# Sliding-window attention with sinks ahead of four dense stages: two 128-column score blocks merged into one of 132

## The chip, the cores and the metric

The kernel runs on one core of one Trainium2 chip. The metric is the device time of one execution in microseconds (us); a smaller one is better. The engines of a core are named as in the profile: PE (TensorE, matrix products, with PEld for its weight loads), DVE (VectorE), ACT (ScalarE), POOL (GpSimd) and SP, which issues most DMAs. Each engine works through its own list of instructions in order.

## The reference

Two batches of 8 heads, 768 positions, 64 values per head. A query attends to the first 4 keys (the sinks) and to the 128 last keys up to its own; the numbers 4 and 128 come as inputs. Then four dense products follow, 512 wide outside and 1024 and 2048 wide inside.

```python
scores = scale * np.matmul(q, k.transpose(0, 1, 3, 2))
keep = is_sink | in_window
scores = np.where(keep, scores, -1000000000.0)
a = np.exp(scores - np.max(scores, axis=-1, keepdims=True))
a = a / (np.sum(a, axis=-1, keepdims=True) + 1e-09)
x = np.matmul(a, v)
h = (x @ w1) * (x @ w2) @ w3 @ w_out
g = softplus(h @ w_in)
out = g @ w_out2
```

## The kernel before

**Stages.** The attention comes first and leaves x for 1536 tokens. Then stage 1 (x times w1 and w2), stage 2 (w3 times w_out), stage 3 and stage 4 (the softplus layer) follow. In these, each fp32 number is split into two parts and each product is three matmuls (lines 153 to 155), which fill PE with matmuls of 512 columns. The weights come as 64-bit words and are decoded on ACT and DVE (lines 179 to 211); the first unit of w1 and w2 is decoded within the attention.

**Attention.** Heads go in pairs, 8 pairs in all, and each head has 6 tiles of 128 queries. For tile i the keys that can count are the 128 of the preceding block, the 4 sinks and the 128 of the tile's own block: 260 columns (`EW`), of which tile 0 uses the last 128. Per pair and tile `score` makes two matmuls, one for each head, into two PSUM tiles. Then per head and tile: `mask` (line 370, DVE) adds the mask, takes the minimum and moves the result to SBUF in one instruction, with a second short one that reads the minimum; `exp` (line 377, ACT) with the row sum; and, once all 6 tiles of a head are there, `total` and `inverse` (lines 383 and 387, DVE), `divide` (line 391, POOL), `turn` (line 403, PE: 11 transposes of 128x128 per head in 3 groups), `turned` (lines 413 and 415: the copy from PSUM, on DVE for g = 2 and, in even heads, g = 1, on ACT for the others), and `pv` (line 438, PE: 7 products per head in two PSUM banks, some of 256 columns and some of 128). The sinks of tiles 2 to 5 go a way of their own: `sink_copy` (POOL, lines 421, 422, 138), `sink_turn`, `sink_turned`, `sink_pv` (lines 447, 450, 457). `x_hi` and `x_lo` (lines 472 and 138) split the result.

**Order.** All these steps are given to a small planner (`Plan`), which writes one fixed order per engine before the program runs. It takes for each step the duration in ns in its `add`, latencies between engines, and a rank: the step's number plus 45 times its value in `PUT_OFF`. At each point it picks the step with the smallest start time plus 0.9 times its rank. So a large positive value sends a step behind others that could start some hundreds of ns later, and a negative one pulls it forward. A step that issues two instructions on DVE costs the planner the sum of the two that it is told. `score` of a tile waits for the masks of the tile before last (4 PSUM tiles), and the step kinds D (decode), vsh and vsl (sink values) and flag are fitted in between.

Of the kernel before, what the change touches and what calls it, by code (L numbers as in the profile page):

```python
# [9 lines left out]
F32 = mybir.dt.float32  # L10
FR = mybir.dt.float32r
# [9 lines left out]
P = 128  # L21
# [6 lines left out]
NSINK = 4  # L28
# [18 lines left out]
PUT_OFF = dict(  # L47
    vsh=1, vs=-20, vsl=-2, nw=-0.5, heat=3, D=16.4, flag=-1,
    S=-1.33, E=(0.31, 1.32), M=(0, -0.01), N=(0.61, 0.14), RC=(0.1, -0.58), C=(0.29, 0.2), T=(0.26, 0.18), P=(0.7, -1.01), K=(0.01, -0.3), PV=0.27, KT=-0.08, KC=-1.39, KV=0.51, XH=0.11, XL=-0.55,
)  # L50

PVS = ([(0, 0, 2), (1, 0, 2), (2, 0, 2), (3, 0, 1)], [(3, 1, 2), (4, 0, 2), (5, 0, 1)])

# [72 lines left out]
class Net:  # L126
# [116 lines left out]
    def mask_steps(self, pool):  # L243
# [4 lines left out]
        col = pool.tile([P, P], I32, name="col")  # L248
        inw, cur, snk, prev, k0, k1, self.m_0 = (
            pool.tile([P, P], F32, name=x) for x in ("inw", "cur", "snk", "prev", "k0", "k1", "m_0")  # L250
        )
        m_1, m_mid = self.m_1, self.m_mid = [pool.tile([P, EW], F32, name=x) for x in ("m_1", "m_mid")]

# [3 lines left out]
        def start():  # L257
            nc.gpsimd.iota(rel, pattern=[[-1, P]], base=0, channel_multiplier=1)
            nc.gpsimd.iota(col, pattern=[[1, P]], base=0, channel_multiplier=0)
            nc.gpsimd.memset(m_1[:, P:KB], -MASKED)  # L260

        return [
# [14 lines left out]
            ("m_0", "DVE", 135, lambda: bias(nc.vector, self.m_0, k0), ("km0",)),  # L277
            ("m_p", "Pool", 268, lambda: bias(nc.gpsimd, m_mid[:, 0:P], prev), ("prev",)),
            ("m_s", "Pool", 164, lambda: bias(nc.gpsimd, m_mid[:, P:KB], snk[:, 0:NSINK]), ("snk",)),
            ("m_c", "ACT", 160, lambda: nc.scalar.copy(m_mid[:, KB:EW], m_1[:, KB:EW]), ("m_1c",)),  # L280
        ]
# [31 lines left out]

    def sink_hi(self, pairs, j):
        if len(self.vshi) == j:
            self.vshi.append(self.ring.tile([P, B * NPAIR, P], FR, tag="u", name=f"vshi{j}", bufs=5))
        self.hi_pool(self.vshi[j][:, pairs], self.vsraw[j][:, pairs])
# [12 lines left out]
    def attention(self, pool, psum):  # L330
# [3 lines left out]

        bufs = dict(qk=3, v=3, e=4, st=4, pt=4)
        shape = dict(qk=[P, S + QT * KB], v=[P, QT, P], e=[P, QT, EW], st=[P, 3, QT], pt=[P, 2 * QT - 1, P])
        users = {}

        def buf(tag, h):

            if (tag, h) not in held:
                held[tag, h] = pool.tile(shape[tag], F32, tag=tag, name=f"{tag}{h}", bufs=bufs[tag])
            return held[tag, h]

# [10 lines left out]
        def tile_columns(i):  # L355
            return slice(KB, EW) if i == 0 else slice(0, EW)

        def score(pair, i):

            o, qk = tile_columns(i), buf("qk", pair)  # L360
# [28 lines left out]
        def divide(h, i):  # L389
            e = buf("e", h)[:, i, tile_columns(i)]  # L390
            nc.gpsimd.tensor_scalar(  # L391
                out=e, in0=e, scalar1=buf("st", h)[:, 2, i : i + 1], scalar2=1.0, op0=ALU.mult, op1=ALU.mult
            )

        def blocks(g):

            return [x for x in ((2 * g, 0), (2 * g, 1), (2 * g + 1, 0), (2 * g + 1, 1)) if x != (0, 0)]

        def turn(h, g):
            held["PT", h, g] = ps = psum.tile([P, 4, P], F32, tag="PT", name=f"ptp{h}_{g}", bufs=2)  # L400
            for j, (t, own) in enumerate(blocks(g)):
                c = slice(KB, EW) if own else slice(0, P)
                nc.tensor.transpose(ps[:, j, :], buf("e", h)[:, t, c], self.ident)

        def on_dve(h, g):

            return g == 2 or g == 1 and h % 2 == 0

        def turned(h, g):
            lo, n = max(4 * g - 1, 0), len(blocks(g))  # L410
            dst, src = buf("pt", h)[:, lo : lo + n, :], held.pop(("PT", h, g))[:, 0:n, :]
            if on_dve(h, g):
                nc.vector.tensor_copy(dst, src)
            else:
                nc.scalar.copy(dst, src)

        def sink_copy(h):
            sk = self.skb[(h // 2) % 2][0]
            src = buf("e", h)[:, 2:QT, P:KB]
# [12 lines left out]
        def pv(pair, bank):  # L432

            for n, (j, s0, s1) in enumerate(PVS[bank]):
                o = (j + s0) * P - bank * CH
                for par in range(2):
                    r = slice(par * D, par * D + D)
                    nc.tensor.matmul(
                        xt(pair, bank)[r, o : o + (s1 - s0) * P], buf("v", pair)[:, j, r],
                        buf("pt", 2 * pair + par)[:, 2 * j + s0 : 2 * j + s1, :],  # L440
                        start=n == 0, stop=False, skip_group_check=True,
                    )
# [64 lines left out]
        for pair in range(B * H // 2):  # L507
# [7 lines left out]
            for i in range(QT):  # L515
# [4 lines left out]
                add("S", "PE", 440 if i else 220, score, pair, i, after=need)  # L520
                m = [] if pair else [(x,) for x in (("m_0",), ("m_1p", "m_1c"), ("m_p", "m_s", "m_c"))[min(i, 2)]]
                for h in heads:
                    add("M", "DVE", 350 if i else 212, mask, h, i, after=[("S", pair, i), *free("e", h), *m])
                    add("E", "ACT", 496 if i else 385, exp, h, i, after=[("M", h, i)])
            users["qk", pair] = [("S", pair, i) for i in range(QT)]
            for h in heads:
                add("N", "DVE", 78, total, h, after=[("E", h, i) for i in range(QT)])
                add("RC", "DVE", 104, inverse, h, after=[("N", h)])
                for i in range(QT):
                    add("C", "Pool", 456 if i else 346, divide, h, i, after=[("RC", h)])  # L530
            old = [("KT", pair - 2)] if pair > 1 else []
            for h in heads:
                for g in range(3):
                    need = [("C", h, 2 * g), ("C", h, 2 * g + 1)]
                    add("T", "PE", 440 if g else 330, turn, h, g, after=need, ring=("PT", ("P", h, g)))
                    to = ("DVE", 602) if on_dve(h, g) else ("ACT", 480 if g else 375)
                    add("P", *to, turned, h, g, after=[("T", h, g), *free("pt", h)])
                add("K", "Pool", 460, sink_copy, h, after=[("C", h, i) for i in range(2, QT)] + old)
                users["e", h] = [("T", h, g) for g in range(3)] + [("K", h)]
            for bank in range(2):  # L540
                need = [("P", h, g) for h in heads for g in ((2,) if bank else (0, 1))] + [("v", pair)]
                need += [("XL", pair - 1, bank)] if pair else []
                add("PV", "PE", 853 if bank else 1493, pv, pair, bank, after=need)
            users["v", pair] = [("PV", pair, b) for b in range(2)]
            for h in heads:
                users["pt", h] = users["v", pair]
            if pair == 0:
# [4 lines left out]
                for part, pairs in enumerate(parts):  # L552
                    ns = 50 + 135 * (pairs.stop - pairs.start)
                    off = 45 * (pairs.start - 1) if part else 0
                    for j in range(2):
                        add("vsh", "Pool", ns, lambda part, j: self.sink_hi(parts[part], j), part, j, after=[last], off=off)
                        last = ("vsh", part, j)
# [427 lines left out]
```

## Time and profile before

| what | value |
|---|---|
| time of three runs | 593.12, 594.55, 595.16 us, median 594.55 us |
| span of the profiled execution | 591.4 us, 8269 instructions |
| what lies around the span, against the median | 3.15 us |
| busy share of the span | PE 99%, PEld 80%, DVE 75%, ACT 60%, POOL 15% |
| chain that ended last | PE 90%, POOL 3%, DVE 3%, DMA 1% |

The span runs from the first to the last instruction; the times of the three runs are those of other executions, so the profiled one's own time is known by its span alone. The busy shares are means over stages with different limits: POOL's 15% is nearly all within the first seventh of the span. PE shows as busy also where its matmuls are spread out by what they wait for, since their ends are modelled.

### The profile page before, as it was taken

Reading aid. Unit: us, or ns where it says so; the run is one execution under the profiler, and the core shown is the slowest. Engines: PE = TensorE matmul, PEld = TensorE weight load, DVE = VectorE, ACT = ScalarE, POOL = GpSimd, SP = SyncE. Lnnn points to the kernel's source line nnn. Section 1 sums busy time; section 2 is a strip of 40 time slices with the busy share of each in tenths; the row PEclk is TensorE's granted clock in tenths of the full one; section 3 lists DMA queues with packets and bytes.
Section 4 is the critical chain, followed back from the end, with each engine's and each line's share of the span. In section 5 each row is a group of like instructions: output and inputs, shape, how many; then the busy total and the mean of one; then the engine's idle time right before and its main releaser. Section 6 shows DMA issues by size and latency. Waiting matters only on the chain.

```text
span 591.4 us, 8269 instructions
## 1 busy us (share of the span) xinstructions
PE 582.7 (99%) x2904; PEld 471.2 (80%) x2904; DVE 441.0 (75%) x916; ACT 354.7 (60%) x720; POOL 89.4 (15%) x213
## 2 busy tenths in 40 slices
PE   9999999999999999999999999999999999999995
PEld 7666678888888888888888788888888888888884
DVE  7989969999998986874999799855545544654553
ACT  6898966766775665654576777643543444444352
POOL 3876840000000000000000101101110111011020
PEclk9999999999999999999999999999999999999999
DMA  8843104444443452440435041000100000100002
GB/s 285 290 146 118 63 9 140 149 164 148 147 169 108 143 174 76 142 141 30 156 134 181 0 133 47 1 0 1 71 1 0 2 0 1 71 1 0 1 0 79
DMA packets 15458, 52.08 MB, mean 88 GB/s; under 512 B 1968, under 2 KB 2480, under 8 KB 15408
## 3 DMA queue, kind: packets, MB, share of 16 engines
q1 hardware_dynamic: 15120, 50.95, 25.3%
q8 instruction: 25, 0.41, 0.3%
q10 hardware_dynamic: 288, 0.52, 0.2%
q14 instruction: 25, 0.20, 0.1%
HBM read 48.32 MB, written 3.15 MB: 87 GB/s over the span
## 4 chain that ended last, share of the span: by engine, by line
PE 90%; POOL 3%; DVE 3%; DMA 1%; issue 0%; ACT 0%; SPq 0%; POOLq 0%; DVEq 0%
PE ab L155 7%; PE ab L153 7%; PE ab L154 7%; PE h L155 7%; PE h L154 7%; PE h L153 7%; PE ox L153 4%; PE ox L155 4%; PE ox L154 4%; PE x2p L155 4%; PE o L154 4%; PE o L155 4%; PE x2p L153 4%; PE o L153 4%; PE x2p L154 4%; POOL e L391 3%
## 5 line engine op out<-in xcount | busy, mean ns | idle before, releaser
L720 POOL TENSOR_SCALAR spu<-spa 128x512 f32<-128x512 f32 (+1 forms) x49 | 30.5, 622 | 463.9 <-ACT spa L719 463.9
L138 DVE TENSOR_TENSOR gl<-spl,gh 128x512 fp32r<-128x512 f32 x47 | 32.6, 693 | 77.0 <-ACT gh L734 76.8
L718 ACT ACTIVATE spa<-h 128x512 f32<-128x512 f32 (+1 forms) x49 | 28.8, 588 | 88.5 <-PE h L155 88.4
L153 PE MATMUL ab<-x,u_w 128*128 128x512 f32 x192 | 74.9, 390 | 0.0
L155 PE MATMUL ab<-x,u_w 128*128 128x512 f32 x192 | 74.9, 390 | 0.0
L154 PE MATMUL ab<-x,u_w 128*128 128x512 f32 x192 | 74.7, 389 | 0.0
L153 PE MATMUL h<-y,w4h 128*128 128x512 f32 x192 | 74.7, 389 | 0.0
L155 PE MATMUL h<-y,w4l 128*128 128x512 f32 x192 | 74.7, 389 | 0.0
L154 PE MATMUL h<-y,w4h 128*128 128x512 f32 x192 | 74.7, 389 | 0.0
L179 ACT ACTIVATE dt_w<-raw_w 128x512 bf16<-128x512 bf16 x64 | 42.4, 670 | 47.5 <-DMA raw_w<-w4d 13.6
L187 DVE SCALAR_TENSOR_TENSOR dc_w<-raw_w,dt_w 128x512 uint16<-128x512 uint16 x64 | 43.5, 688 | 12.9 <-ACT dt_w L182 11.9
L391 POOL TENSOR_SCALAR e<-e,st 128x260 f32<-128x260 f32 (+1 forms) x96 | 46.0, 498 | 20.2 <-DVE st L387 11.5
L377 ACT ACTIVATE e<-e,st 128x260 f32<-128x260 f32 (+1 forms) x96 | 46.7, 490 | 3.9 <-DVE st L370 3.1
L182 ACT ACTIVATE dt_w<-dt_w,rebias 128x512 uint16<-128x512 uint16 x64 | 45.6, 721 | 1.4
L725 DVE SCALAR_TENSOR_TENSOR spu<-spu,spa 128x512 f32<-128x512 f32 (+1 forms) x49 | 33.3, 680 | 17.3 <-ACT spl L723 17.2
L154 PEld LDWEIGHTS h<-y,w4h 128*128 128x128 f32 x192 | 36.0, 188 | 7.5
L155 PEld LDWEIGHTS ab<-x,u_w 128*128 128x128 f32 x192 | 36.0, 188 | 7.5
L153 PEld LDWEIGHTS h<-y,w4h 128*128 128x128 f32 x192 | 36.0, 188 | 7.5
L154 PEld LDWEIGHTS ab<-x,u_w 128*128 128x128 f32 x192 | 36.0, 188 | 7.5
L155 PEld LDWEIGHTS h<-y,w4l 128*128 128x128 f32 x192 | 36.1, 188 | 7.4
L153 PEld LDWEIGHTS ab<-x,u_w 128*128 128x128 f32 x192 | 36.0, 188 | 7.3
L723 ACT ACTIVATE spl<-spu 128x512 f32<-128x512 f32 (+1 forms) x49 | 30.5, 624 | 18.9 <-POOL spu L720 18.2
(137 smaller groups left out, 1341.5 us busy)
## 6 DMA issues: line engine op xcount, KB each, us to landing
raw_w<-w4d SPq DMA_DIRECT2D x32, 511.8 KB, 3.9
raw_w<-w SPq DMA_DIRECT2D x16, 511.8 KB, 4.0
raw_w<-w3t SPq DMA_DIRECT2D x16, 511.8 KB, 3.9
qk<-qk SPq DMA_DIRECT2D x7, 780.0 KB, 6.3
raw_wo<-wod SPq DMA_DIRECT2D x8, 511.8 KB, 3.6
v<-v SPq DMA_DIRECT2D x8, 384.0 KB, 5.3
out<-os SPq DMA_DIRECT2D x10, 256.0 KB, 2.3
vsraw<-vsink SPq DMA_DIRECT2D x2, 512.0 KB, 10.2
```

Source lines behind the costliest of these rows:

```text
L138: return engine.tensor_tensor(out=lo, in0=x, in1=hi.bitcast(F32), op=ALU.subtract)
L153: nc.tensor.matmul(ps, lhs[0], rhs[0], start=start, stop=False)
L154: nc.tensor.matmul(ps, lhs[0], rhs[1], start=False, stop=False)
L155: nc.tensor.matmul(ps, lhs[1], rhs[0], start=False, stop=stop)
L179: return nc.scalar.activation(t.bitcast(BF), x["top"].bitcast(BF), AF.Abs)
L182: return nc.scalar.activation(x["t"], x["t"], AF.Relu, bias=self.rebias[:, 0:1], scale=8.0)
L187: nc.vector.scalar_tensor_tensor(out=c, in0=x["top"], scalar=0x8000, in1=t, op0=ALU.bitwise_and, op1=ALU.bitwise_or)
L377: nc.scalar.activation(e, e, AF.Exp, bias=st[:, 0, i : i + 1], scale=-1.0, accum_out=st[:, 1, i : i + 1])
L391: nc.gpsimd.tensor_scalar(out=e, in0=e, scalar1=buf("st", h)[:, 2, i : i + 1], scalar2=1.0, op0=ALU.mult, op1=ALU.mult)
L720: nc.gpsimd.tensor_scalar(out=u[:, c], in0=a[:, c], scalar1=1.0, scalar2=1.0, op0=ALU.add, op1=ALU.mult)
L723: nc.scalar.activation(l[:, c], u[:, c], AF.Ln)
L725: nc.vector.scalar_tensor_tensor(out=u[:, c], in0=u[:, c], scalar=1.0, in1=a[:, c], op0=ALU.subtract, op1=ALU.subtract)
```

## The change

For tiles 2 to 5 the columns of the preceding block and of the own block are put over each other: for a window of 128 a key of the own block counts where it is not later than the query, and a key of the preceding block counts exactly where the own one at the same place is later. `mask` first copies the preceding block's scores over the own ones in PSUM where the own key is later (`copy_predicated` with a new 0/1 table `later`), and then masks 132 columns (4 sinks and 128 merged) in place of 260. `exp` and `divide` take 132 columns. `turn` makes 7 transposes per head in 2 groups, `turned` is always on ACT. Behind it a new DVE step `split` (U) multiplies the 4 merged blocks by a 0/1 table `below`, which leaves the preceding block's part alone. In `pv`, the merged block is multiplied with the own block's v, and the part with a difference of two v blocks that the new POOL step `change` (V) makes once per pair; that is 10 products per head, 9 of 128 columns and one of 256. The buffers are allocated once instead of in turn, `vshi` has memory of its own, `m_p` on POOL goes and `m_c` moves from ACT to DVE, and all values of `PUT_OFF` are other ones.

```diff
 PUT_OFF = dict(
-    vsh=1, vs=-20, vsl=-2, nw=-0.5, heat=3, D=16.4, flag=-1,
...
+    XH=(25.63, 15.72), XL=(15.94, 2.87), qk=(30.22, -94.01), flag=70.73, D=(31.31, 23.58),
 )
-PVS = ([(0, 0, 2), (1, 0, 2), (2, 0, 2), (3, 0, 1)], [(3, 1, 2), (4, 0, 2), (5, 0, 1)])
+PVS = (
+    [("v", 0, 0, 2, 0), ("v", 1, 2, 1, 1), ("v", 2, 3, 1, 2), ("v", 3, 4, 1, 3), ("d", 2, 7, 1, 2), ("d", 3, 8, 1, 3)],
+    [("v", 4, 5, 1, 4), ("v", 5, 6, 1, 5), ("d", 4, 9, 1, 4), ("d", 5, 10, 1, 5)],
+)
...
+            ("km2", "DVE", 202, lambda: nc.vector.tensor_tensor(out=k2, in0=cur, in1=prev, op=ALU.max), ("cur", "prev")),
...
+            ("m_c", "DVE", 135, lambda: bias(nc.vector, m_mid[:, NSINK:KB], k2), ("km2",)),
+            ("later", "DVE", 196, lambda: nc.vector.tensor_scalar(
+                out=self.later, in0=rel, scalar1=0.0, scalar2=None, op0=ALU.is_lt), ("iota",)),
+            ("below", "Pool", 1200, below, ("iota",)),
...
         def mask(h, i):
             o = tile_columns(i)
-            m = (self.m_0, self.m_1, self.m_mid)[min(i, 2)]
+            m, s = (self.m_0, self.m_1, self.m_mid)[min(i, 2)], held.pop(("S", h, i))
+            if i > 1:
+                nc.vector.copy_predicated(s[:, KB:EW], self.later, s[:, 0:P])
             nc.vector.tensor_tensor_reduce(
-                out=buf("e", h)[:, i, o], in0=held.pop(("S", h, i))[:, o], in1=m, scale=-SCALE, scalar=3.0e38,
+                out=exponents(h, i), in0=s[:, o], in1=m, scale=-SCALE, scalar=3.0e38,
...
         def on_dve(h, g):
-            return g == 2 or g == 1 and h % 2 == 0
+            return False
...
+        def split(h):
+            pt = buf("pt", h)
+            nc.vector.tensor_tensor(out=pt[:, 7:11, :], in0=pt[:, 3:7, :], in1=self.below, op=ALU.mult)
+
+        def change(pair):
+            v = buf("v", pair)
+            nc.gpsimd.tensor_tensor(out=buf("d", pair), in0=v[:, 1 : QT - 1, :], in1=v[:, 2:QT, :], op=ALU.subtract)
...
-                    add("M", "DVE", 350 if i else 212, mask, h, i, after=[("S", pair, i), *free("e", h), *m])
-                    add("E", "ACT", 496 if i else 385, exp, h, i, after=[("M", h, i)])
+                    add("M", "DVE", (212, 350, 415)[min(i, 2)], mask, h, i, after=[("S", pair, i), *free("e", h), *m])
+                    add("E", "ACT", (396, 496, 400)[min(i, 2)], exp, h, i, after=[("M", h, i)])
...
+                add("U", "DVE", 602, split, h, after=[("P", h, 1)] + ([] if h else [("below",)]))
...
+            add("V", "Pool", 900, change, pair, after=[("v", pair), *free("d", pair)])
```

## Rows read from the trace of the kernel before

**Rows 1.** Busy time by stage: us, then PE, PEld, DVE, ACT, POOL, clock, DMA.

```profile
0.00:6.00 6.00, 5.01 (x50) 4.91 (x52) 3.18 (x24) 1.58 (x2) 2.32 (x14) 1.00 0.62 156
6.00:75.00 69.00, 67.91 (x567) 46.29 (x567) 63.87 (x270) 64.04 (x235) 50.13 (x132) 1.00 0.52 180
75.00:85.50 10.50, 10.26 (x91) 7.22 (x87) 5.34 (x14) 6.39 (x17) 6.54 (x18) 1.00 0.01 2
85.50:591.40 505.90, 499.55 (x2203) 412.82 (x2201) 368.64 (x610) 282.68 (x467) 30.46 (x49) 1.00 0.23 77
```

**Rows 2.** Chain that ended last, in order of time: start us, us, what.

```profile
28.23 2.53 PE xt L438 x28
...
82.62 2.53 PE xt L438 x28
...
85.52 0.43 PE ab L153
```

**Rows 3.** DVE from 6 to 75 us by form: busy us, mean ns, idle before.

```profile
L370 DVE CUSTOM_DVE_ANT_0 e<-s,m_mid 128x260 f32<-128x260 f32 x64 | 23.7, 423 | 0.3
L413 DVE COPY pt<-ptp 128x512 f32<-128x512 f32 x21 | 14.4, 687 | 0.4 <-PE ptp L403 0.4
L370 DVE CUSTOM_DVE_ANT_0 e<-s,m 128x128 f32<-128x128 f32 x16 | 4.1, 288 | 2.1 <-PE s L365 2.0
...
L201 DVE TENSOR_TENSOR dr_w<-dc_w,dr_w 128x512 f32<-128x512 bf16 x2 | 1.3, 668 | 0.0
L196 DVE SCALAR_TENSOR_TENSOR dr_w<-raw_w,dt_w 128x512 f32<-128x512 uint32 x2 | 1.3, 668 | 0.0
L187 DVE SCALAR_TENSOR_TENSOR dc_w<-raw_w,dt_w 128x512 uint16<-128x512 uint16 x2 | 1.3, 668 | 0.0
```

**Rows 4.** Timeline of DVE, two masks in a row: start us, us.

```profile
62.16 0.43 DVE L370 CUSTOM_DVE_ANT_0 e<-s,m_mid 128x260 f32<-128x260 f32 x1
...
62.51 0.43 DVE L370 CUSTOM_DVE_ANT_0 e<-s,m_mid 128x260 f32<-128x260 f32 x1
```

**Rows 5.** Timeline of DVE while the mask tables are made.

```profile
3.53 0.28 DVE L267 SCALAR_TENSOR_TENSOR cur<-rel,inw 128x128 f32<-128x128 int32 x1
3.73 0.28 DVE L271 TENSOR_SCALAR prev<-rel,val 128x128 f32<-128x128 int32 x1
...
4.27 0.38 DVE L276 TENSOR_TENSOR k<-cur,snk 128x128 f32<-128x128 f32 x1
4.68 0.29 DVE L255 TENSOR_SCALAR m<-k 128x128 f32<-128x128 f32 x1
```

**Rows 6.** Timeline of DVE, a decode within the attention.

```profile
47.60 0.65 DVE L196 SCALAR_TENSOR_TENSOR dr_w<-raw_w,dt_w 128x512 f32<-128x512 uint32 x1
48.17 0.69 DVE L187 SCALAR_TENSOR_TENSOR dc_w<-raw_w,dt_w 128x512 uint16<-128x512 uint16 x1
48.89 0.29 DVE L190 TENSOR_SCALAR dt_w<-dc_w 128x512 uint16<-128x512 uint16 x1
```

**Rows 7.** Timeline of DVE in stage 4, the second reading what the first wrote.

```profile
400.70 0.69 DVE L725 SCALAR_TENSOR_TENSOR spu<-spu,spa 128x512 f32<-128x512 f32 x1 [1.84 <-ACT spl L723]
401.43 0.69 DVE L728 SCALAR_TENSOR_TENSOR spu<-h,spu 128x512 f32<-128x512 f32 x1
```

**Rows 8.** PE from 6 to 75 us by form, as rows 3.

```profile
L403 PE MATMUL ptp<-ident,e 128*128 128x128 f32 x154 | 22.9, 282 | 0.3 <-ACT pt L415 0.2
L438 PE MATMUL xt<-pt,v 128*64 128x256 f32 x102 | 13.6, 386 | 0.0
L438 PE MATMUL xt<-pt,v 128*64 128x128 f32 x72 | 6.0, 273 | 0.0
```

**Rows 9.** ACT from 6 to 77 us by form, as rows 3.

```profile
L377 ACT ACTIVATE e<-e,st 128x260 f32<-128x260 f32 x80 | 40.3, 507 | 1.3 <-DVE st L370 1.3
L377 ACT ACTIVATE e<-e,st 128x128 f32<-128x128 f32 x16 | 6.5, 406 | 2.6 <-DVE st L370 1.9 <-DVE st L387 0.7
L415 ACT COPY pt<-ptp 128x512 f32<-128x512 f32 x7 | 4.0, 567 | 0.0
```

**Rows 10.** POOL, divides from 6 to 75 us by form; then a 512-column one of stage 4 (page, part 5).

```profile
L391 POOL TENSOR_SCALAR e<-e,st 128x260 f32<-128x260 f32 x70 | 33.0, 487 | 0.0
...
L720 POOL TENSOR_SCALAR spu<-spa 128x512 f32<-128x512 f32 (+1 forms) x49 | 30.5, 622 | 463.9 <-ACT spa L719 463.9
```

More of the change, by code (lines that the diff above doesn't have):

```diff
@@ L248, in mask_steps @@
         col = pool.tile([P, P], I32, name="col")
-        inw, cur, snk, prev, k0, k1, self.m_0 = (
-            pool.tile([P, P], F32, name=x) for x in ("inw", "cur", "snk", "prev", "k0", "k1", "m_0")
-        )
-        m_1, m_mid = self.m_1, self.m_mid = [pool.tile([P, EW], F32, name=x) for x in ("m_1", "m_mid")]
+        inw, cur, snk, prev, k0, k1, k2, self.m_0 = (
+            pool.tile([P, P], F32, name=x) for x in ("inw", "cur", "snk", "prev", "k0", "k1", "k2", "m_0")
+        )
+        m_1 = self.m_1 = pool.tile([P, EW], F32, name="m_1")
+        m_mid = self.m_mid = pool.tile([P, KB], F32, name="m_mid")
+        self.later = pool.tile([P, P], I32, name="later")
+        self.below = pool.tile([P, QT - 2, P], F32, name="below")
         def bias(engine, dst, keep):
@@ L260, in start, with below @@
             nc.gpsimd.memset(m_1[:, P:KB], -MASKED)
+        def below():
+            for j in range(QT - 2):
+                nc.gpsimd.tensor_scalar(
+                    out=self.below[:, j, :], in0=rel, scalar1=0.0, scalar2=1.0, op0=ALU.is_gt, op1=ALU.mult
+                )
         return [
@@ L333, in attention, with exponents @@
         held = {}
-        bufs = dict(qk=3, v=3, e=4, st=4, pt=4)
-        shape = dict(qk=[P, S + QT * KB], v=[P, QT, P], e=[P, QT, EW], st=[P, 3, QT], pt=[P, 2 * QT - 1, P])
+        bufs = dict(qk=3, v=3, d=2, e=4, f=4, st=4, pt=4)
+        shape = dict(
+            qk=[P, S + QT * KB], v=[P, QT, P], d=[P, QT - 2, P], e=[P, 2, EW], f=[P, QT - 2, KB],
+            st=[P, 3, QT], pt=[P, 2 * QT - 1, P],
+        )
         users = {}
+        tiles = {t: [pool.tile(shape[t], F32, name=f"{t}{i}") for i in range(bufs[t])] for t in bufs}
         def buf(tag, h):
-            if (tag, h) not in held:
-                held[tag, h] = pool.tile(shape[tag], F32, tag=tag, name=f"{tag}{h}", bufs=bufs[tag])
-            return held[tag, h]
+            return tiles[tag][h % bufs[tag]]
+        def exponents(h, i, own=False):
+            if i > 1:
+                return buf("f", h)[:, i - 2, NSINK if own else 0 : KB]
+            return buf("e", h)[:, i, tile_columns(0 if own else i)]
         def free(tag, h):
@@ L389, in divide @@
         def divide(h, i):
[L390 removed]
+            e = exponents(h, i)
             nc.gpsimd.tensor_scalar(
@@ L395, in blocks @@
         def blocks(g):
-            return [x for x in ((2 * g, 0), (2 * g, 1), (2 * g + 1, 0), (2 * g + 1, 1)) if x != (0, 0)]
+            return [(i, 1) for i in range(2, QT)] if g else [(0, 1), (1, 0), (1, 1)]
         def turn(h, g):
@@ L432, in pv @@
         def pv(pair, bank):
-            for n, (j, s0, s1) in enumerate(PVS[bank]):
-                o = (j + s0) * P - bank * CH
+            for n, (kind, j, s, m, t) in enumerate(PVS[bank]):
+                o = t * P - bank * CH
                 for par in range(2):
@@ L529, in attention @@
                 for i in range(QT):
-                    add("C", "Pool", 456 if i else 346, divide, h, i, after=[("RC", h)])
+                    add("C", "Pool", (350, 459, 353)[min(i, 2)], divide, h, i, after=[("RC", h)])
             old = [("KT", pair - 2)] if pair > 1 else []
             for h in heads:
-                for g in range(3):
-                    need = [("C", h, 2 * g), ("C", h, 2 * g + 1)]
+                for g in range(2):
+                    need = [("C", h, i) for i, _ in blocks(g)]
                     add("T", "PE", 440 if g else 330, turn, h, g, after=need, ring=("PT", ("P", h, g)))
-                    to = ("DVE", 602) if on_dve(h, g) else ("ACT", 480 if g else 375)
+                    to = ("DVE", 602 if g else 470) if on_dve(h, g) else ("ACT", 470 if g else 362)
                     add("P", *to, turned, h, g, after=[("T", h, g), *free("pt", h)])
+                add("U", "DVE", 602, split, h, after=[("P", h, 1)] + ([] if h else [("below",)]))
                 add("K", "Pool", 460, sink_copy, h, after=[("C", h, i) for i in range(2, QT)] + old)
-                users["e", h] = [("T", h, g) for g in range(3)] + [("K", h)]
+                users["e", h] = [("T", h, g) for g in range(2)] + [("K", h)]
+            add("V", "Pool", 900, change, pair, after=[("v", pair), *free("d", pair)])
             for bank in range(2):
-                need = [("P", h, g) for h in heads for g in ((2,) if bank else (0, 1))] + [("v", pair)]
-                need += [("XL", pair - 1, bank)] if pair else []
+                need = [("U", h) for h in heads] + [("P", h, 0) for h in heads if not bank] + [("V", pair)]
+                need += [("XL", pair - 1, bank)] if pair else [("heat", 63)]
                 add("PV", "PE", 853 if bank else 1493, pv, pair, bank, after=need)
-            users["v", pair] = [("PV", pair, b) for b in range(2)]
+            users["v", pair] = users["d", pair] = [("PV", pair, b) for b in range(2)]
             for h in heads:
@@ L555, in attention @@
                     for j in range(2):
-                        add("vsh", "Pool", ns, lambda part, j: self.sink_hi(parts[part], j), part, j, after=[last], off=off)
+                        add("vsh", "Pool", ns, lambda part, j: self.sink_hi(pool, parts[part], j), part, j, after=[last], off=off)
                         last = ("vsh", part, j)
```

36 lines of the change are left out of this document (20 added, 16 removed).

## The prediction

> **What bounds the kernel now.** I first cut the span into stages [rows 1]. From 85.5 us to the end, 505.9 us, PE is busy for 499.55 us with the dense stages, which the change does not touch. So the change is worth what it does to the first 85.5 us, where the chain that ended last passes from the products with v to stage 1 at 85.52 us [rows 2]. The reader should see there that no single engine has room: between 6 and 75 us, 69.0 us, PE shows 67.91 us, ACT 64.04, DVE 63.87, POOL 50.13. The products with v start at 28.23 us in pair 1 and at 82.62 us in pair 7 [rows 2]: 54.39 us for six pairs, 9.07 us per pair. The granted clock is 1.00 in every stage (the 2.4 GHz level), and I count no change of it.
>
> The idle time of DVE in that stretch is 69.0 - 63.87 = 5.1 us, that of ACT 5.0 us, that of PE 1.1 us. PE therefore sets today's pace, with DVE and ACT only some 0.5 us per pair behind. An engine that gets more work than its idle time becomes the new bound. That is the question for DVE.
>
> **PE, ACT and POOL lose work.** A transpose takes 22.9 / 154 = 0.149 us [rows 8]; 4 fewer per head are 8 x 0.149 = 1.2 us per pair. The products with v keep their columns (11 blocks per head) but come as more matmuls. From the same rows an instruction of 256 columns takes 13.6 / 102 = 0.133 us and one of 128 takes 6.0 / 72 = 0.083. There are two instructions per matmul and two heads: 16 and 12 of them per pair today, 4 and 36 afterwards, so 3.52 in place of 3.12 us, +0.4. The lower bound is 0, if time goes by columns alone. PE falls to 9.07 - 1.2 + 0.0 to 0.4, at most 8.3 us per pair.
>
> On ACT, 8 of a pair's 12 exponentials go from 260 to 132 columns, near the 128-column form: 507 - 406 = 0.10 us less each [rows 9], -0.8 us. One copy of 512 columns per pair comes over from DVE, 0.57 less an overlap of about 0.08. Net -0.3 us per pair.
>
> On POOL a divide of 260 columns takes 33.0 / 70 = 0.47 us [rows 10]. With 132 columns it lies between half of that and no gain; I take -0.1 us for each of 8. The new V is one two-input instruction of 512 columns. The nearest row is a one-input one with 0.622 us [rows 10]; bounds 0.62 and, for twice the inputs, twice that, 1.24. I take 0.9. POOL is idle for 18.9 of 69 us, and V needs only a loaded v, so this stays hidden. So does the making of `below` at the start, and the 0.3 us that ACT gains.
>
> **DVE is where it is decided.** A mask of 260 columns costs 62.51 - 62.16 = 0.35 us from start to start [rows 4]. Instructions overlap by 0.43 - 0.35 = 0.08. For 128 columns that gives 0.288 - 0.08 = 0.21 [rows 3], so 0.21 for 132.
>
> The predicated copy of 128 columns does not occur before. The nearest rows are 128-column instructions of DVE with 3.73 - 3.53 = 0.20 us [rows 5]. Bounds: 0.20, and 0.30 by the slower one of that group (0.38 busy less 0.08). I take 0.20.
>
> Then comes a price that is easily left out. The mask reads what the copy wrote, on the same engine, and nothing stands between the two in the order. Two instructions of 512 columns with no such tie start 48.17 - 47.60 = 0.57 us apart; the next one, which reads what the second wrote, starts 48.89 - 48.17 = 0.72 later [rows 6], 0.12 to 0.15 more. In stage 4 the tied pair is 401.43 - 400.70 = 0.73 us apart [rows 7], 0.12 more than 0.69 - 0.08. At 128 columns a tied pair stands 4.68 - 4.27 = 0.41 apart against 0.20 [rows 5], 0.21 more. I take 0.13, with 0 and 0.21 as bounds. None of these rows shows DVE writing to PSUM.
>
> The Trainium skill, VectorE: DVE Perf Modes, section The DRAIN you can't avoid, says that a semaphore between chained DVE instructions costs nothing extra, since the pipeline is flushed in any case. By that the new mask would be 0.41 us and the sum that of rival (a) below. The trace disagrees [rows 6, 7]: 0.12 us at least.
>
> The new mask step is 0.20 + 0.13 + 0.21 = 0.54 us in place of 0.35: +0.19 us for each of the 64 steps of tiles 2 to 5, +12.2 us. The copies from PSUM that leave DVE save 21 x (0.687 - 0.08) = 12.8 us up to 75 us [rows 3]. U comes in their place: two SBUF inputs, 512 columns, like line 201 with 0.668 - 0.08 = 0.59 us [rows 3]; 14 of them up to there, +8.3 us. DVE's sum is 12.2 - 12.8 + 8.3 = +7.7 us, so 71.6 us of work where 69.0 us of time were. **DVE becomes the bound**, and ACT and PE wait for it.
>
> What takes some of it back. First, idle time: of the 5.1 us I take 2.1 to remain, since what DVE waits for now comes earlier; -3.0 us (bounds -1 and -4). Second, the decode of the first weight unit. Its three long DVE instructions are 3 x 1.3 = 3.9 us of this stretch [rows 3]. D goes from 16.4 to 31.3 and 23.6 in PUT_OFF, so the planner fills it only into longer gaps, and more of it falls behind 75 us, where DVE is busy for 5.34 of 10.5 us [rows 1]. I take -2.3 (bounds 0 and -3.9). The planner orders with 415 ns for the mask, about 0.20 + 0.21 with no wait in it, so it holds DVE for lighter than it is; I use that number for the order alone.
>
> **Start and tail.** Ahead of the first masks DVE is busy for 3.18 of 6 us [rows 1]. It gets three more instructions of 0.20, two of them tied, and the flag's go later: 0 to +0.9, I take +0.3. In the tail POOL's divides set the way to the last products: 6.54 us of work from 75 to 85.5 [rows 1], of which 8 x 0.1 goes. The last head's way to its products gains one step, U, with 0.6 us and a wait, which the last two divides (tiles 0 and 1) can hide. I take -0.5 (bounds -1.5 and +0.6).
>
> **The sum**: +0.3 + 7.7 - 3.0 - 2.3 - 0.5 = +2.2 us. The profiled span of 591.4 us lies 3.15 us under the median of 594.55; what lies around it does not change, so I add to the median: 596.8 us, 0.4% slower. A measurement of this kernel can tell about 0.3%, 1.8 us, from no change. With the bounds of idle time, decode, start and tail the case runs from about 594 to 600.
>
> **Rivals.**
> (a) The copy and the mask run back to back, with no wait. Then DVE's sum is 7.7 - 64 x 0.13 = -0.6, its work stays at about today's, and PE's 1.2 and ACT's 0.3 us per pair become usable: +0.3 - 0.6 - 3.0 - 2.3 - 0.5 = -6.1. ACT's own room, 0.3 x 7 = 2.1 us, the 2.3 us of decode, which leave it too, and the tail allow some -4.5: 590. For it: nothing in the trace shows a DVE instruction on PSUM in place. Against: every tied pair of [rows 5 to 7]. It is also what the section of the Trainium skill named above (VectorE: DVE Perf Modes, The DRAIN you can't avoid) would give. Should the wait be real but the decode leave the stretch wholly and DVE's idle time shrink by 4, we get +0.3 + 7.7 - 4.0 - 3.9 - 0.5 = -0.4: no change, within the forecast's case.
> (b) Writing and reading back through PSUM costs more than the rows in SBUF: 0.21 in place of 0.13, and nothing to hide it, since DVE is already the bound. That adds 64 x 0.08 = 5.1 us: 602. It decides as soon as DVE has no idle time left. For it: the widest tied pair [rows 5]. Against: that pair ran beside POOL's work on the tables.
> (c) PE stays the bound, because the narrow products cost more than the transposes save. By the rows that is +0.4 against -1.2 us per pair; I give it nothing of its own.
>
> **How the numbers follow.** The forecast's case (wait of about 0.13, DVE the bound) gets 0.57, (a) 0.25, (b) 0.18. Of the forecast's case, 0.33 is slower by over 0.3%, 0.19 within, 0.05 faster; of (a) 0.22 faster and 0.03 within; (b) is all slower. That makes 0.27 faster, 0.22 same, 0.51 slower. The range reaches from (a) at 590 to (b) at 602; the likeliest case alone has 594 to 600.
>
> **What would show it.** In the profile of the changed kernel: 64 predicated copies with 0.20 us and a mask of 0.21 whose start lies about 0.33 after its copy's; DVE busy 90% or more of the attention with its waits for PE smaller; PE with visible gaps there, released by DVE; 112 transposes in place of 176; exponentials of 0.40; U 16 times 0.6 us; V hidden on POOL; stage 1 starting near 87.7 us in place of 85.5. A copy-to-mask distance near 0.20, or stage 1 starting before 84 us, makes the forecast wrong in favour of (a); a distance over 0.4 speaks for (b).

## The result, and the profile after

The changed kernel takes 602.99 us (median of 4 runs, 600.45 to 605.01) against 594.6 us for the kernel before (median of 4). The ratio is 1.0135, 95% interval 1.0105 to 1.0164: slower by 1.35%, or 8.0 us of 594.5. The forecast was +2.2 us, slower, with 602 as the upper end of the range. The sign was right; the size was too small and the median lies outside the range. The profiled execution has a span of 600.8 us, 9.4 more than the one of before. In what follows a worth is a difference of ratios times 594.5 us, unless a median is named.

By stage, the windows of after; columns as in [rows 1]:

```profile
0.00:6.00 6.00, 5.03 (x46) 4.84 (x48) 3.10 (x20) 1.28 (x1) 4.66 (x17) 1.00 0.54 146
6.00:75.00 69.00, 68.23 (x529) 47.17 (x529) 63.13 (x302) 57.52 (x225) 51.41 (x132) 0.98 0.47 165
75.00:85.50 10.50, 9.01 (x104) 6.80 (x103) 10.02 (x30) 7.21 (x23) 8.88 (x17) 1.00 0.13 39
85.50:92.80 7.30, 6.61 (x57) 5.13 (x55) 5.95 (x12) 5.35 (x11) 3.59 (x11) 0.77 0.19 59
92.80:600.80 508.00, 501.42 (x2210) 414.06 (x2208) 369.08 (x615) 281.05 (x467) 30.30 (x49) 1.00 0.24 77
```

The dense stages take 508.0 us where they took 505.9 [rows 1], and 1.6 of these 2.1 us are seven matmuls of stage 1, told below. The rest of the loss lies ahead of 92.8 us. Before, the last mask started at 74.1 us and stage 1 ran without a break from 85.45. Now these are 78.2 and 92.76 us. So the way to the last mask is 4.1 us longer and the tail behind it 14.6 us in place of 11.35, 3.2 longer.

DVE's groups from the start to 96 us (busy, mean ns, idle before), which answer to [rows 3]:

```profile
L405 DVE CUSTOM_DVE_ANT_0 f<-s,m_mid 128x132 f32<-128x132 f32 x64 | 18.9, 295 | 3.2
L404 DVE COPY_PREDICATED s<-later,s 128x128 f32<-128x128 int32 x64 | 18.5, 289 | 1.5 <-PE s L397 1.4
L455 DVE TENSOR_TENSOR pt<-pt,below 128x512 f32<-128x512 f32 x16 | 15.9, 994 | 0.9 <-ACT pt L450 0.9
```

DVE's timeline at a mask step, which answers to [rows 4]:

```profile
57.33 0.29 DVE L404 COPY_PREDICATED s<-later,s 128x128 f32<-128x128 int32 x1
57.66 0.29 DVE L405 CUSTOM_DVE_ANT_0 f<-s,m_mid 128x132 f32<-128x132 f32 x1
57.88 0.08 DVE L405 DVE_READ_ACCUMULATOR2_ANT st<- 128x1 f32 x1
57.88 0.29 DVE L404 COPY_PREDICATED s<-later,s 128x128 f32<-128x128 int32 x1
```

The mask starts 0.33 us behind its copy, the next copy 0.22 behind the mask: 0.55 us per step, where 0.54 was forecast. In DVE's timeline 55 of the 64 masks start 0.30 to 0.34 us behind their copy and nine 0.42 to 0.44 us; the mean is 0.34. The idle time of 3.2 us ahead of the masks, 64 times 0.05 us, has no releaser in the profile, as if the engine waited for itself; experiment 2 tests that. The overlap of neighbours is lost besides.

What was not foreseen is in the third group: U takes 0.994 us in place of 0.668 busy. POOL's group of V, then two U's on DVE's timeline and the V beside the second on POOL's:

```profile
L460 POOL TENSOR_TENSOR d<-v 128x512 f32<-128x512 f32 x8 | 10.2, 1270 | 6.9 <-DMA v<-v 6.9
```

```profile
58.76 0.68 DVE L455 TENSOR_TENSOR pt<-pt,below 128x512 f32<-128x512 f32 x1
...
65.64 1.70 DVE L455 TENSOR_TENSOR pt<-pt,below 128x512 f32<-128x512 f32 x1
67.27 0.28 DVE L404 COPY_PREDICATED s<-later,s 128x128 f32<-128x128 int32 x1
```

```profile
65.52 1.27 POOL L460 TENSOR_TENSOR d<-v 128x512 f32<-128x512 f32 x1
```

The same instruction takes 0.68 us alone and 1.70 us when it starts 0.12 us behind a V. It ends 0.55 us after V does, nearly what it needs alone: it hardly advances while V runs. Five of the 16 U's (at 45.6, 55.3, 65.6, 75.5 and 88.0 us) take 1.37 to 1.70 us, each started 0.1 to 0.5 us behind a V; they make 7.69 us of U's 15.9, 4.3 more than five of 0.68. All five end 0.54 to 0.55 us after their V.

The tail: POOL's divides of the last two heads in the chain of waits of before, then those of after with the last links, which answer to [rows 2]; then the windows of 2 us there:

```profile
75.64 1.37 POOL e L391 x3
77.14 3.13 POOL e L391 x7
...
80.73 0.93 POOL e L391 x2
```

```profile
79.31 1.65 POOL e L426 x2
80.96 1.40 POOL f L426 x4
82.36 2.19 POOL e L426 x2
84.55 2.41 POOL f L426 x4
...
88.25 4.22 PE xt L483 x40
92.46 0.37 PE xt L502 x4
92.83 0.43 PE ab L164
```

```profile
86.00:88.00 2.00, 1.31 (x7) 0.54 (x5) 0.78 (x4) 1.31 (x4) 2.00 (x10) 1.00 0.02 8
88.00:90.00 2.00, 2.00 (x17) 1.60 (x19) 2.00 (x3) 1.69 (x4) 1.09 (x1) 0.60 0.04 8
90.00:92.00 2.00, 2.00 (x24) 2.00 (x22) 1.98 (x4) 1.51 (x4) 0.00 (x0) 0.54 0.11 39
```

Three things are seen. The last products take 4.22 us; before it was 2.53 [rows 2]. Their granted clock is 0.54 to 0.60, close to the 1.2 GHz level, after two microseconds in which PE was busy for 1.31. POOL's twelve divides of the last two heads take 7.65 us in place of 5.43, though eight of them are narrower: the last four take 2.41 us, four in a row at 80.96 only 1.40. And stage 1 has to start from nothing at 92.8: PE's timeline of before shows what it did in the same place:

```profile
77.95 0.48 PE L153 MATMUL ab<-x,u_w 128*128 128x512 f32 x1
78.27 0.40 PE L154 MATMUL ab<-x,u_w 128*128 128x512 f32 x1
78.77 0.61 PE L403 MATMUL ptp<-ident,e 128*128 128x128 f32 x3
79.14 0.48 PE L155 MATMUL ab<-x,u_w 128*128 128x512 f32 x1
```

Seven of stage 1's matmuls ran in the gaps of the attention's end, 7 x 0.23 = 1.6 us of work done early, which also kept PE going. After, there is none, because the weights' decode on DVE, whose first instruction started at 38.7 us before (those of [rows 6] are later ones), now begins behind the last mask, at 79.6 us.

So 9.4 us of span are 4.1 to the last mask, 3.2 in the tail, 1.6 of lost early matmuls, and 0.5 not placed.

### The profile page after: what moved, and what is told of

Read it like the earlier page. It is cut to its first block, busy times and chain, and to the rows that moved or that the text cites. A ratio compares the mean times of both kernels' runs of the same rounds, so it can differ in the third digit from the quotient of the medians.

```text
span 600.8 us, 8514 instructions
## 1 busy us (share of the span) xinstructions
PE 590.3 (98%) x2936; PEld 478.0 (80%) x2936; DVE 451.3 (75%) x975; ACT 352.4 (59%) x727; POOL 98.8 (16%) x224
## 4 chain that ended last, share of the span: by engine, by line
PE 95%; DVE 2%; POOL 2%; ACT 1%; issue 0%; DVEq 0%; ACTq 0%
PE ab L164 7%; PE ab L166 7%; PE ab L165 7%; PE h L166 7%; PE h L164 7%; PE h L165 7%; PE s L397 6%; PE ox L164 4%; PE ox L166 4%; PE o L166 4%; PE x2p L164 4%; PE o L164 4%; PE x2p L165 4%; PE ox L165 4%; PE x2p L166 4%; PE o L165 4%
## 5 line engine op out<-in xcount | busy, mean ns | idle before, releaser
L149 DVE TENSOR_TENSOR gl<-spl,gh 128x512 fp32r<-128x512 f32 x47 | 32.6, 693 | 77.1 <-ACT gh L781 76.9
L198 DVE SCALAR_TENSOR_TENSOR dc_w<-raw_w,dt_w 128x512 uint16<-128x512 uint16 x64 | 43.5, 688 | 11.6 <-ACT dt_w L193 10.5
L770 ACT ACTIVATE spl<-spu 128x512 f32<-128x512 f32 (+1 forms) x49 | 30.4, 623 | 18.9 <-POOL spu L767 18.1
L397 PE MATMUL s<-qk 64*128 64x260 f32 (+1 forms) x192 | 40.6, 409 | 0.8 <-DVE st L405 0.3
L164 PE MATMUL x2p<-ab,w 128*128 128x512 f32 x96 | 37.3, 389 | 0.0
```

Of the source, the lines that this page charges most:

```text
L149: return engine.tensor_tensor(out=lo, in0=x, in1=hi.bitcast(F32), op=ALU.subtract)
L164: nc.tensor.matmul(ps, lhs[0], rhs[0], start=start, stop=False)
L198: nc.vector.scalar_tensor_tensor(out=c, in0=x["top"], scalar=0x8000, in1=t, op0=ALU.bitwise_and, op1=ALU.bitwise_or)
L770: nc.scalar.activation(l[:, c], u[:, c], AF.Ln)
```

## The experiments

Edits are given against the changed kernel.

**1. V's work taken out (v_two), and given to DVE (v_dve).**

```diff
 def change(pair):
+    if pair > 1:
+        return
     v = buf("v", pair)
-    nc.gpsimd.tensor_tensor(out=buf("d", pair), ...
+    nc.vector.tensor_tensor(out=buf("d", pair), ...
```

The first two added lines are v_two, the last line is v_dve. In v_two the later pairs multiply with the differences of the first two pairs, so part of the computation is left out. The expectations speak of seven long U's in the changed kernel; five is the count.

> V is made for the first two pairs only; the later pairs multiply with those differences (part of the computation left out). All else and the order stay as in the changed kernel (603.0 us). Theory 1 (two-input work of POOL and DVE on SBUF holds each other up): U's mean of 0.99 us falls below 0.75, six of the seven U of 1.4 to 1.7 us vanish, and DVE, the bound, gains about 6 x 0.8 = 4.8 us: 598 to 599.5. Rival (U is long for a reason of its own, and V is hidden as I had predicted): U stays near 1.0 us and the time at 602 to 604.

> V is issued on DVE at the same place of the order instead of POOL. Theory 1: DVE gets 8 x 0.6 = 4.8 us more of its own, but the seven U that wait for V lose 0.8 us each, 5.6 us; the result is near that of the changed kernel, 601 to 603.5, with no U over 0.9 us. Rival (V on POOL costs nothing): 4 to 5 us slower, 607 to 608.

Measured: v_two 596.59 us, ratio 1.0046 [1.0031, 1.0060]; v_dve 602.59 us, 1.0148 [1.0124, 1.0173]. U in v_two and, below it, U and V in v_dve, DVE's groups:

```profile
L455 DVE TENSOR_TENSOR pt<-pt,below 128x512 f32<-128x512 f32 x16 | 11.4, 711 | 0.9 <-ACT pt L450 0.9
```

```profile
L455 DVE TENSOR_TENSOR pt<-pt,below 128x512 f32<-128x512 f32 x16 | 11.8, 737 | 1.0 <-ACT pt L450 1.0
...
L460 DVE TENSOR_TENSOR d<-v 128x512 f32<-128x512 f32 x8 | 6.0, 756 | 0.9 <-DMA v<-v 0.9
```

Without six of the eight V's, U falls to 0.711 us, 4.5 us less over 16, and the time by 0.0089 x 594.5 = 5.3 us. With V on DVE, U falls too, and DVE has 6.0 us of V instead; the time stays within the intervals. So V on POOL costs this kernel about as much as if DVE did it.

**2. The wait between copy and mask (copies_first).** Both heads' copies go ahead of both masks, so that another instruction stands between a copy and the mask that reads it; nothing else changes.

```diff
-            if i > 1:
-                nc.vector.copy_predicated(s[:, KB:EW], self.later, s[:, 0:P])
+            if i > 1 and ("S", h ^ 1, i) in held:
+                for t in (s, held["S", h ^ 1, i]):
+                    nc.vector.copy_predicated(t[:, KB:EW], self.later, t[:, 0:P])
```

> For tiles 2 to 5 both heads' predicated copies go ahead of the first head's mask, so that another instruction stands between each copy and the mask that reads it. Theory 1 (the tied start costs 0.11 us each and DVE sets the pace): the two copies and masks of a tile take 0.86 us in place of 1.10, 32 x 0.24 = 7.7 us less on DVE, and the time falls by 4 to 7.5 us: 595.5 to 599. Rival (the pace is set by waits between engines and by the end of the attention, not by DVE's work): less than 2 us, 601 to 603.

Measured: 594.57 us, 1.0013 [0.9995, 1.0031], 7.2 us less than the changed kernel and no different from before. DVE's groups, then its timeline:

```profile
L405 DVE CUSTOM_DVE_ANT_0 f<-s,m_mid 128x132 f32<-128x132 f32 x64 | 16.5, 289 | 0.0
L455 DVE TENSOR_TENSOR pt<-pt,below 128x512 f32<-128x512 f32 x16 | 15.5, 971 | 0.8 <-ACT pt L450 0.6
L404 DVE COPY_PREDICATED s<-later,s 128x128 f32<-128x128 int32 x64 | 15.5, 288 | 0.7 <-PE s L397 0.6
```

```profile
61.16 0.49 DVE L404 COPY_PREDICATED s<-later,s 128x128 f32<-128x128 int32 x2
61.56 0.29 DVE L405 CUSTOM_DVE_ANT_0 f<-s,m_mid 128x132 f32<-128x132 f32 x1
61.77 0.09 DVE L405 DVE_READ_ACCUMULATOR2_ANT st<- 128x1 f32 x1
61.77 0.29 DVE L405 CUSTOM_DVE_ANT_0 f<-s,m_mid 128x132 f32<-128x132 f32 x1
61.99 0.09 DVE L405 DVE_READ_ACCUMULATOR2_ANT st<- 128x1 f32 x1
```

Two steps take 61.99 - 61.16 = 0.83 us in place of 1.10, and the 3.2 us of idle time ahead of the masks are 0.0. The work is the same to the instruction, so the wait is what most of the time was paid for. Not all of the gain need be the wait: in the profiled executions DVE also waits for PE's scores once near 15 to 17 us, 1.41 us in the changed kernel (PE's granted clock from 12 to 16 us is 0.67) and 0.60 us here (1.00). The last mask starts at 71.2 us, 2.9 earlier than before, but stage 1 only at 85.3: the tail takes 14.1 us, and the lead is lost there.

**3. Both (copies_v_two).** The edits of v_two and copies_first together.

> Both heads' copies ahead of the masks, and V for the first two pairs only (the later differences are left out of the computation). If the tied start and U's wait for V are two separate costs on DVE, both fall out of the time: 594.6 - 6 = 587.5 to 590. Rival (either alone already frees DVE, and POOL, PE or the end of the attention sets the time then): 592.5 to 595.

Measured: 591.21 us, 0.9952 [0.9933, 0.9972]. The two costs are separate: without the V's another 0.0061 x 594.5 = 3.6 us go from copies_first, where 5.3 went from the changed kernel. With the intervals of the ratios both values are uncertain by 1.6 to 2 us, so whether the costs add up in full is not shown. Without six of the V's this kernel is not a candidate.

**4. U reads PSUM (u_psum, u_psum_copies, u_psum_ring).** U takes the group before its copy to SBUF, so that one of its inputs is not from SBUF. u_psum_copies adds copies_first; u_psum_ring adds copies_first's edit to the planner's knowledge that U frees the buffer.

```diff
+            if g:
+                held["U", h] = src
...
-        nc.vector.tensor_tensor(out=pt[:, 7:11, :], in0=pt[:, 3:7, :], in1=self.below, op=ALU.mult)
+        nc.vector.tensor_tensor(out=pt[:, 7:11, :], in0=held.pop(("U", h)), in1=self.below, op=ALU.mult)
...
-    ring=("PT", ("P", h, g)))
+    ring=("PT", ("U", h) if g else ("P", h, g)))
```

The last pair of lines is in u_psum_ring alone.

> U reads the turned scores where PE left them, in PSUM, instead of ACT's copy in SBUF; only the table below then comes from SBUF. V stays on POOL, the order is that of the changed kernel (603.0 us). Theory 1 (U and V get in each other's way because both read two tensors from SBUF): every U takes 0.6 to 0.7 us also beside V, and the time is near that without most of the V, 596 to 599. Rival (V holds up whatever DVE reads from SBUF, so one input is enough): U beside V stays over 1.2 us and the time at 601 to 604.

> U from PSUM as in u_psum and both heads' copies ahead of the masks as in copies_first, nothing else. If both costs lie on DVE and DVE still is the bound after either is gone, they add up: 603.0 - 8.4 - 5 = 588 to 591. Rival (with one of them gone, the end of the attention or another engine sets the time): 592.5 to 595.

> As u_psum_copies (598.8 us), but the planner is told that the PSUM buffer of the transposes is free only behind U, and plans anew. Theory 1 (u_psum lost to PE's waits for that buffer, which the plan did not know of): PE's waits for U shrink and the time is 590 to 595. Rival (two such buffers are too few when U holds one, in any order): 597 to 601.

Measured: 605.30 us, 1.0206 [1.0187, 1.0225]; 598.79 us, 1.0101 [1.0082, 1.0119]; 604.77 us, 1.0173 [1.0155, 1.0191]. All three miss in time. U's own durations in u_psum (lowest, median, highest), and what PE waits for there from 6 to 90 us (us, times, longest):

```profile
L457 DVE TENSOR_TENSOR pt<-ptp,below x16: 648/686/691, 20.5 to 93.5; 128x512 f32<-128x512 f32 x16
```

```profile
PE skp L494 <- DVE pt L457: 3.3, 2, 2.0
PE ptp L438 <- DVE pt L457: 2.5, 3, 0.9
```

No U is over 0.691 us any more, though V runs as before: with one input in PSUM, U is not held up. But U now holds the transposes' PSUM buffer, and PE, which ran ahead of DVE, waits for it. That this new wait eats the gain is likely, but not shown: in u_psum_ring, whose order is planned anew with the buffer's true end, no wait of PE for U is left in the profile, and the time is no better.

**5. V put elsewhere on POOL (copies_v_moved, copies_v).** Both with copies_first, the planner's order kept but for V. copies_v_moved issues V behind the K step (the sinks' copy on POOL) of the pair before; there V of some pairs stands ahead of its load and takes an earlier pair's v, so its time is not that of the whole computation. copies_v issues V as soon as its load, that K step and the products two pairs before have been issued.

```diff
-        for s in plan.order(...):
-            s["emit"]()
+        for s in steps:
+            ...
+            done.add(s["key"])
+            for key in list(vs):
+                if ("v", key[1]) in done and ("K", 2 * key[1] - 1) in done and (key[1] < 2 or ("PV", key[1] - 2, 1) in done):
+                    vs.pop(key)["emit"]()
```

> Both copies ahead, and each V but the first issued on POOL right behind the sink copies of the pair before, where POOL waits for the next reciprocal, and no longer behind the pair's own divides. All is computed. Theory 1 (what V costs is its meeting with U and its place in the last pair): at most three U over 0.9 us, 588.5 to 591.5, under both kernels. Rival (V meets another U there, or delays the divides): 593.5 to 596.

> copies_first with each V but the first moved up on POOL: behind the sink copies of the pair before, the load of its v and the products that free its buffer, whichever is last. All is computed. Theory 1 (V's cost is its meeting with U on SBUF): U's mean falls from 0.97 to below 0.8 us and the time to 590.5 to 592.5, near copies_v_two (591.2). Rival (moved up, V holds up POOL's divides or waits for its buffer): 594 to 597.

Measured: 596.95 us, 1.0055 [1.0040, 1.0071]; 599.34 us, 1.0103 [1.0089, 1.0118]: both slower than copies_first. U, and what PE's weight loads wait for, in copies_v:

```profile
L455 DVE TENSOR_TENSOR pt<-pt,below 128x512 f32<-128x512 f32 x16 | 11.6, 728 | 2.5 <-ACT pt L450 2.4
```

```profile
PEld ptp L438 <- POOL f L426: 9.5, 30, 0.6
PEld ptp L438 <- POOL e L426: 6.2, 13, 1.6
```

The meeting is gone (0.728 us), but V's 1.27 us now stand ahead of divides, and the transposes wait for the divides of tiles 2 to 5 for 9.5 us, 30 times, against 5.3 us, 18 times in copies_first. That this is the loss was not tested by itself. That there is a place on POOL where V hurts neither was not found; whether one exists stays open.

**6. The decode (decode_early, copies_decode).** decode_early sets D back to 16.4 in PUT_OFF; copies_decode is copies_first with the order kept and only D's 16 steps placed behind the RC steps (the reciprocals) of heads 5 to 13.

```diff
-    XH=(25.63, 15.72), XL=(15.94, 2.87), qk=(30.22, -94.01), flag=70.73, D=(31.31, 23.58),
+    XH=(25.63, 15.72), XL=(15.94, 2.87), qk=(30.22, -94.01), flag=70.73, D=16.4,
```

```diff
+        for k in range(8):
+            at.setdefault(("RC", 5 + k), []).append(("D", 0, k))
+            at.setdefault(("RC", 6 + k), []).append(("D", 1, k))
+        for s in steps:
+            if s["key"] not in late:
+                s["emit"]()
+            for k in at.get(s["key"], ()):
+                late[k]["emit"]()
```

> Only D in PUT_OFF goes back to 16.4, as before the change, so the first weight unit is decoded within the attention again. Theory 1 (the late decode holds up POOL's last divides and leaves PE without the 7 matmuls of stage 1 that ran in the gaps before): stage 1's matmuls appear ahead of the last products again, POOL's divides in the tail take 0.47 us, PE's clock stays at 1.00, and the time falls by 2 to 4 us: 599 to 601. Rival (my prediction: the decode adds to DVE's work where DVE is the bound, so the masks end as much later as the tail gets shorter): 602 to 606.

> As copies_first (594.6 us), with the order left as it is but for the 16 steps of the first weight unit's decode, which go one by one behind the reciprocals of heads 5 to 13 instead of into the end of the attention. Theory 1 (late decode: its two-input instructions lengthen POOL's last divides, and PE lacks stage 1's matmuls as a filler): POOL's last four divides take 1.4 us in place of 2.9, some of stage 1's matmuls appear ahead of the last products, and the time is 592 to 594. Rival (my prediction: the 5 us of decode on DVE delay the masks by as much as the end gains): 594.5 to 598.

Measured: 610.80 us, 1.0280 [1.0263, 1.0297]; 596.56 us, 1.0061 [1.0044, 1.0078]. The first is no clean test: the one value reorders the whole plan, and from 6 to 75 us PE shows 63.24 us of 69.0 at a granted clock of 0.85. The second is: it costs 2.9 us against copies_first, though stage 1's first matmul comes at 75.92 us. The last mask starts at 76.2 in place of 71.2. Behind it the tail is as short as before: from the last mask to the unbroken run of stage 1 it is 11.7 us (11.35 before, 14.1 in copies_first), POOL's twelve last divides take 5.1 us and the last products 2.55. So most of the tail's growth goes with the late decode; v_two, which keeps it but lacks the last V, has 12.9 us. Still, here an early decode takes more from a DVE that is the bound than it gives back in the tail.

**7. PE kept at work in the tail (tail_warm, copies_warm).** Idle products of a constant tile: four with each transpose of group 1 (in tail_warm in the last head, in copies_warm in the last two heads) and ten ahead of the last sink transpose.

```diff
+                if (h, g) == (H * B - 1, 1):
+                    warm(4)
...
+            if pair == H * B // 2 - 1:
+                warm(10)
```

> The changed kernel with idle 128-column bf16 matmuls on PE where it waits at the end of the attention: four ahead of each of the last head's last four transposes, ten ahead of the last sink transpose. Theory 1 (PE's gaps at 86 to 88 us let the granted clock fall to 0.50 for the last products, which took 4.2 us in place of 2.5): the clock stays at 1.00 from 86 to 93 us, the last products take 2.6 us, and the time falls by 1 to 2 us: 601 to 602. Rival (the last products wait for U, not for the clock): no change, 602.5 to 604.

> copies_first (594.6 us) with the idle matmuls of tail_warm, here ahead of each of the last four transposes of both heads of the last pair and ten ahead of the last sink transpose. If the clock that fell to 0.50 from 76 to 79.5 us lay on the path to the last products, as in the changed kernel, 1 to 2 us go: 592.5 to 593.5. Rival (there POOL's divides of the last head set the end, and the products of the pair before have time): 594 to 595.

Measured: 600.68 us, 1.0113 [1.0096, 1.0131]; 595.70 us, 1.0038 [1.0024, 1.0052]. The windows of tail_warm, beside those of after above:

```profile
86.00:88.00 2.00, 2.00 (x32) 1.84 (x28) 0.76 (x2) 1.18 (x3) 2.00 (x10) 1.00 0.00 0
88.00:90.00 2.00, 2.00 (x26) 1.56 (x27) 1.98 (x3) 1.81 (x4) 0.97 (x1) 1.00 0.00 0
90.00:92.00 2.00, 2.00 (x27) 1.66 (x24) 1.93 (x4) 1.54 (x4) 0.00 (x0) 1.00 0.13 35
```

With PE busy throughout, the clock stays at 1.00, the last products take 3.0 us and stage 1 starts at 91.4 us in place of 92.76. The pair before takes 2.55 us for the same 40 instructions; in the last pair the chain breaks at 89.57 us, where U, beside V, has just ended. So of the 1.7 us that the last products grew, 1.2 are the clock and nearly all of the rest is this wait. In time that is 1.3 us by the ratios and 2.3 by the medians, with overlapping intervals: likely, not certain. In copies_warm the clock is mended too, from 0.51 to 1.00 between 76 and 79.5 us, and nothing is gained: its chain of waits passes there through DVE's decode, `84.94 0.48 DVE dc_w L198` and `85.54 0.68 DVE u_w L149`.

**8. Sums (all_three, copies_warm_v).** all_three is u_psum_copies with copies_decode's order, copies_warm_v is copies_warm with copies_v's.

> U from PSUM, both copies ahead of the masks, and the decode spread over heads 5 to 13. Theory 1: 586 to 589.5, below both kernels. Rival (decode within the stretch costs more than it gives at the end): above u_psum_copies by 1 us or more.

> Both edits together. If each gives what theory 1 says: 589 to 591.5, below the kernel before by over 0.3%. Rival: no better than the better of the two.

Measured: 604.65 us, 1.0193 [1.0176, 1.0210]; 599.75 us, 1.0108 [1.0093, 1.0124]. Misses, as their parts were. No version that does all the work beat both kernels; the best, copies_first, equals before.

## Why the prediction was wrong in size and right in direction

**What held.** DVE became the bound: 66.03 us busy of 72 from 6 to 78 us. The forecast's visible gaps of PE did not come: its one wait for a mask there is 0.3 us. The mask step was forecast as 0.54 us and is mostly 0.55; two copies in a row start 0.20 us apart (experiment 2); the exponentials of 132 columns take 0.402 us; the 40 narrow products of a pair take 2.55 us at full clock where 28 took 2.53, the lower bound of their term. The start is not shown: the first mask comes at 6.6 us in place of 6.0, behind 1.1 us of waiting for PE's scores, and in seven other runs whose kernels start alike at 5.6 to 7.2 us. The wait of 0.13 us between copy and mask, taken from [rows 6, 7], was the heart of the forecast. copies_first puts a price on it: 64 x (1.10 - 0.83) / 2 = 8.6 us of DVE, and with it goes 7.2 us of time. The Trainium skill, VectorE: DVE Perf Modes, section The DRAIN you can't avoid, says that a semaphore between chained DVE instructions costs nothing extra. The trace of this pair disagrees: 0.32 to 0.33 us from start to start for most, against 0.20 between two copies.

**The step that failed: "V needs only a loaded v, so this stays hidden", with U at 0.59 us.** I looked for idle time on POOL, found 18.9 us, and took a hidden instruction for a free one. V takes 1.27 us, just over the upper bound of 1.24, and while it runs a U hardly advances: U is 0.994 us in place of 0.668 busy, 16 x 0.326 = 5.2 us. v_two takes 4.5 of them away, and the time falls by 5.3 us by the ratios. (The text ahead of the prediction puts nearly all of POOL's 15% into the first seventh of the span; by [rows 1] 59.0 us lie there and 30.5 us in the dense stages, which changes nothing in this stretch.) The Trainium skill, GPSIMD Engine Reference, section Specifications, says that the SBUF interfaces are shared with VectorE, with contention for DVE instructions that have two SBUF inputs. The trace agrees, 0.68 against 1.70 us, and u_psum shows the other half, 0.691 us at most with one input from PSUM. No rival held this mechanism.

**The second step that failed: the tail, "-0.5 us".** It was +3.2 and 1.6 us of early matmuls lost. By place, the way to the last mask grew by 4.1 us where the terms gave +0.3 + 7.7 - 3.0 - 2.3 = +2.7; most of the miss lies in the tail. The decode's move behind 75 us was priced for DVE alone, as a gain of 2.3 us; in the tail it took the work with which PE had filled its gaps, and its instructions with two SBUF inputs run beside POOL's divides, which set the way to the last products. These were forecast 0.8 us shorter and are 7.65 - 5.43 = 2.2 longer. The last products are 4.22 - 2.53 = 1.7 longer, 1.2 of it by the lower granted clock (experiment 7); the other links are 0.6 shorter, which leaves 3.3, the 3.2 but for rounding. copies_decode, without the late decode, has the short divides, the short products and a tail of 11.7 us. I had counted no change of the clock, since every row of before had 1.00; besides the tail it fell from 12 to 16 us, to 0.67.

**Where errors cancelled.** Without V (v_two) the time is 596.59 us, the forecast nearly to the digit, but not by its terms. There the last mask starts at 74.3 us, +0.2 where the terms up to there gave +2.7. All of the decode left the stretch (-3.9, the bound, in place of -2.3), and 13 U's fall into it, not 14 (-0.6). That explains 2.2 of the 2.5. The tail gives it back: 12.9 us in place of 11.35, +1.6, and the 1.6 us of early matmuls.

**The rivals.** (a) fell: the wait is there. (b) named 602 us, near the result, but for a distance of over 0.4 us between copy and mask, and it is that in nine of 64 pairs, 0.30 to 0.34 in the others. The likeness is chance. Its price came from a misread row: the first instruction of the pair in [rows 5] is itself 0.38 us long, so of the 0.41 us only 0.41 - (0.38 - 0.08) = 0.11 is the tie, as in [rows 6, 7]. (c) fell.

**Open.** Whether V's share differs between 5.3 us alone and 3.6 us behind copies_first, or only by noise. What the new order costs by itself: all values of PUT_OFF changed with the edit, no run keeps the old ones, and decode_early shows one value to be worth 0.0145 x 594.5 = 8.6 us. A clean early decode in the changed kernel's own order was not tried. Why nine masks start 0.1 us later than the others was not looked into.

## What to carry to other kernels

Before work is called hidden on an idle engine, look at what the bounding engine does at that moment: here an instruction of POOL that reads SBUF and one of DVE with two SBUF inputs took nearly the sum of their times (U and V side by side 1.82 us, for 0.68 and 1.27 alone), and it held for POOL's divides with one tensor too. Where an instruction reads what the one ahead of it on the same engine wrote, put an independent one between them; here that edit was worth 7.2 us of 594.5. And price a step that is moved out of a full stretch at the place where it goes too, with the work that it released there.

## What the runs showed of the hardware

- A U of 512 columns takes 0.65 to 0.69 us alone and up to 1.70 us behind a V of 1.27 us; read from PSUM, never more than 0.69. Starting first does not save it: in copies_first a U that starts beside a divide, 0.25 us ahead of V, takes 2.07 us.
- POOL is held up as well: four divides, 1.40 us elsewhere, take 2.41 us while DVE runs U and two-input steps of the decode; with U from PSUM (u_psum) the 64 divides of 132 columns fall from 0.435 to 0.398 us in the mean.
- A copy in PSUM and the mask that reads it start 0.30 to 0.34 us apart in 55 of 64 pairs, against 0.20 to 0.22 for neighbours with no tie. That is 0.12 us for the tie, as between SBUF tensors in [rows 6, 7].
- The granted clock fell from 1.00 to 0.54 to 0.60 for the last products after PE had been busy for 1.31 of 2 us, and stayed at 1.00 with idle products in the gap (tail_warm).
